# A state-space layer with a SwiGLU branch on one core: five engine streams written with and without a block around them

## The chip, the cores and the metric

The kernel runs on one core of a Trainium2 chip. A core has five engines with an instruction stream each: TensorE (PE in the profile), VectorE (DVE), ScalarE (ACT), GpSimd (POOL) and SyncE (SP). [...] Here SP does no arithmetic: it issues the large transfers to the DMA engines and waits for them. The metric is the device time of one execution in microseconds (us). The kernel before takes 178.64 us (median of 3 runs, 178.61 to 178.97).

## The reference

The input x has 2048 rows of 512. Each row is normalised, and the result goes through two branches whose outputs are added to x:

```python
def _A_ref(x, ...):                       # diagonal complex state space
    Lam_bar = jnp.exp(dt * Lam)           # dt = exp(log_dt)
    B_bar = ((Lam_bar - 1.0) / Lam)[:, None] * Bmat
    Bu = jnp.einsum("bld,pd->blp", x + 0j, B_bar)
    for t in range(L):
        h = Lam_bar[None, :] * h + Bu[:, t, :]
        hs.append(h)
    y = 2.0 * jnp.einsum("blp,dp->bld", hseq, Cmat).real + x * Dskip[None, None, :]
    return y

def _B_ref(x, w_gate, w_up, w_down):
    g = _silu(x @ w_gate)
    u = x @ w_up
    return (g * u) @ w_down

xn = _layernorm(x, axis=-1)
return x + _A_ref(xn, ...) + _B_ref(xn, w_gate, w_up, w_down)
```

There are 512 complex states, and the hidden width of the SwiGLU branch is 1376. Inputs and output are bfloat16.

## The kernel before

The 2048 rows are handled in four chunks of 512. For each chunk VectorE or ScalarE normalises the rows, the rows are transposed (by TensorE in the first chunk, by DMA later), TensorE multiplies them by the gate and up weights (line 807, and line 835 for the first six gate tiles of chunk 0) and by the two parts of B (line 952), ScalarE takes the results out of PSUM (lines 820, 902, 956), VectorE multiplies gate and up (line 904), rotates the states, scans them over time (line 994) and rotates them back, and TensorE adds both branches into one PSUM bank with the down weights (line 1041) and the C weights (line 1054). At the end of a row tile VectorE adds the residual (line 1066) and SP issues the transfer of the tile to the output (the helper at line 438). The last row tile of the last chunk is cut into columns of 256, 128 and 128, so the last addition is 128 columns wide and the last transfer 256.

Nothing is issued directly while this is written down. Every operation is entered into a graph as a task with an engine, its reads, its writes and an estimated cost. At the end `_schedule` orders the tasks of each engine (TensorE and SP keep the order in which they were entered), and `_plan` gives every task the semaphore level it signals and the waits it needs. `_emit` (line 263) then goes through one engine's list and writes each task's waits and its instructions to that engine. A wait that can't ride on an instruction is an instruction of its own (line 266).

The transfers to the output that nobody waits for share one semaphore. `_plan` returns it with its last level as `end_sem, end_lvl`, and SP waits for that level after its last task; this is the kernel's only wait for its own output. The other four engines have no last wait of that sort.

All five lists are written inside a block object, opened at line 306 before the first buffer is laid out. Its five decorated functions (lines 1137 to 1156) each open a section of the program for one engine. A block adds three things: a branch on each engine from the main section into its own section, a branch from there to a common closing section, and in this closing section a barrier of all five engines. The barrier has two sides. ACT, PE, DVE and SP each execute a DRAIN, which raises a gathering semaphore once that engine's earlier work is complete, and then wait for a release; POOL drains, waits until the gathering semaphore has been raised four times, and then raises the release semaphore by four. The profile puts these instructions at line 305, the line of the `with` statement.

A barrier of the same make stands at the start of the program. It belongs to the making of the program object (line 1170), after four small memsets of constants, and has nothing to do with the block. Behind it come, on each engine, the first tasks: on SP and ACT the first transfers (line 438), on PE a run of matmuls on constants (line 508), on POOL memsets (from line 488).

ScalarE's table of activation functions is loaded by an instruction that the program gets when it is completed, ahead of the first activation (line 501).

Of the kernel before, what the change touches and what calls it, by code (L numbers as in the profile page):

```python
# [262 lines left out]
def _emit(eng_obj, stream):  # L263
    for t in stream:
        for sem, val in t.waits:
            eng_obj.wait_ge(sem, val)
        inst = t.fn(eng_obj)
        if t.sem is not None and (t.nsig or t.dma):
            inst.then_inc(t.sem, 16 if t.dma else 1)


def bass_parallel_sum__ssm_conv_s5__swiglu_ffn__prompt_kernel(
# [30 lines left out]
    g = _Graph()  # L303
    es = ExitStack()
    with es:
        block = es.enter_context(nc.Block())

        def sb(name, shape, dt):
            return es.enter_context(nc.sbuf_tensor(name, shape, dt))

# [173 lines left out]
        def loads_wd():  # L484
# [17 lines left out]
              name="act_warm", est=220, prio=1e6)  # L502
# [628 lines left out]
        streams = _schedule(g.tasks, engs)  # L1131
# [2 lines left out]
        eng_sems = {e: new_sem("sem_" + e) for e in engs if e != "sp"}  # L1134
        end_sem, end_lvl = _plan(g.tasks, streams, new_sem, eng_sems)

        @block.sync
        def _(e):
            _emit(e, streams["sp"])
            e.wait_ge(end_sem, end_lvl)  # L1140

        @block.tensor
        def _(e):
            _emit(e, streams["pe"])

        @block.scalar
        def _(e):
            _emit(e, streams["act"])

        @block.vector  # L1150
        def _(e):
            _emit(e, streams["dve"])

        @block.gpsimd
        def _(e):
            _emit(e, streams["pool"])


# [26 lines left out]
```

## Time and profile before

| | |
|---|---|
| median of 3 runs | 178.64 us (178.61 to 178.97) |
| the profiled execution: its own time | 178.72 us |
| the profiled execution: first to last instruction of the program (span) | 177.0 us |
| granted TensorE clock, mean | 1.000 |
| TensorE matmuls, busy | 173.4 us, 98% of the span |
| VectorE, busy | 162.0 us, 92% |
| ScalarE, busy | 101.4 us, 57% |
| GpSimd, busy | 15.1 us, 9% |
| instructions in the trace | 2634 |

The span runs from the first instruction of the program on any engine, at 0.0, to the end of the last one. The execution's own time is longer, because it also covers what the runtime does around the program; the page has no rows for that part. In the rows, an engine's name with a q (SPq, PEq) stands for its sequencer: branches, drains, semaphore waits and the issuing of transfers are done there, take no time on the engine itself, and are not counted as busy. "x" with a number is how often a row's instruction occurs.

### The profile page before, as it was taken

What the parts mean: (1) busy time and instruction counts of PE and PEld (TensorE: products, weight loads), DVE (VectorE), ACT (ScalarE), POOL (GpSimd) and SP (SyncE); (2) the same over time, 40 slices, a digit from 0 to 9 for tenths busy, and PEclk for the clock granted to TensorE, in tenths of its full rate; (3) what the DMA queues carried; (4) which work ended last, traced back from release to release, by engine and by line L of the source; (5) the groups of instructions that cost most, each with busy time, mean ns of one, the idle gap of its engine ahead of it and who ended that gap; (6) DMA issues with size and microseconds to landing.
All of it is one profiled execution on the core that took longest, in us unless ns stands there. A gap on an engine that the chain in (4) does not pass through costs nothing.

```text
span 177.0 us, 2634 instructions
## 1 busy us (share of the span) xinstructions
PE 173.4 (98%) x948; PEld 86.5 (49%) x956; DVE 162.0 (92%) x342; ACT 101.4 (57%) x201; POOL 15.1 (9%) x38
## 2 busy tenths in 40 slices
PE   8999999999999999999999999999999999999994
PEld 2884644455444444446444444445544444444743
DVE  3687899999989979999999999999999999999983
ACT  4679999999998739896598500620666610000000
POOL 6630500000000280000000000000000000000000
DMA  5999669793000700002008000001110000001012
GB/s 149 267 362 250 118 122 171 181 343 131 0 4 0 148 0 0 0 16 77 32 0 150 0 4 0 0 0 59 59 33 0 2 0 0 0 4 59 30 59 89
DMA packets 25092, 12.91 MB, mean 73 GB/s; under 512 B 17304, under 2 KB 25080, under 8 KB 25080
## 3 DMA queue, kind: packets, MB, share of 16 engines
q1 hardware_dynamic: 25056, 12.75, 28.4%
q8 instruction: 7, 0.11, 0.3%
q14 instruction: 5, 0.04, 0.1%
q10 hardware_dynamic: 24, 0.00, 0.0%
HBM read 6.46 MB, written 2.10 MB: 48 GB/s over the span
## 4 chain that ended last, share of the span: by engine, by line
PE 98%; issue 0%; DVE 0%
PE pb L807 36%; PE pb L1041 21%; PE pb L952 16%; PE pb L1054 16%; PE pb L835 3%; PE pb L917 3%; PE pb L508 2%; PE pb L642 1%; DVE osb L1066 0%; PE pb L517 0%
## 5 line engine op out<-in xcount | busy, mean ns | idle before, releaser
L807 PE MATMUL pb<-xnT,wgu 128*128 128x512 bf16 x296 | 64.7, 379 | 0.0
L807 PEld LDWEIGHTS pb<-xnT,wgu 128*128 128x128 bf16 x296 | 28.9, 98 | 33.7
L994 DVE TENSOR_TENSOR_SCAN vq<-sm,car,vq 128x512 bf16<-128x512 f32 x32 | 39.7, 1274 | 0.1
L1041 PE MATMUL pb<-wd,hT 128*128 128x512 bf16 (+3 forms) x194 | 38.1, 355 | 0.2
L1041 PEld LDWEIGHTS pb<-wd,hT 128*128 128x128 bf16 (+1 forms) x198 | 18.5, 98 | 19.9
L952 PE MATMUL pb<-xnT,BT 128*128 128x512 bf16 x128 | 28.1, 379 | 0.0
L1054 PE MATMUL pb<-W,hss 128*128 128x512 bf16 (+2 forms) x140 | 27.8, 355 | 0.2
L956 ACT ACTIVATE u_sb<-pb 128x512 bf16<-128x512 f32 x32 | 18.6, 594 | 13.2 <-PE pb L952 12.4
L902 ACT ACTIVATE uf<-pb 128x512 bf16<-128x512 f32 x40 | 23.5, 606 | 4.3 <-PE pb L807 2.7
L820 ACT ACTIVATE sg<-pb 128x512 bf16<-128x512 f32 x34 | 20.4, 600 | 2.8 <-PE pb L807 2.6
L1054 PEld LDWEIGHTS pb<-W,hss 128*128 128x128 bf16 x144 | 13.5, 98 | 14.2
L952 PEld LDWEIGHTS pb<-xnT,BT 128*128 128x128 bf16 x128 | 12.5, 98 | 15.1
L904 DVE TENSOR_TENSOR hT<-sg,uf 128x512 bf16<-128x512 bf16 x40 | 16.5, 418 | 2.1 <-ACT uf L902 1.3
L1066 DVE TENSOR_TENSOR osb<-pb,x_sb 128x512 bf16<-128x512 f32 (+2 forms) x18 | 11.2, 627 | 1.7 <-PE pb L1054 1.2
L985 DVE TENSOR_TENSOR scrA<-u_sb,cosT 128x1024 bf16<-128x1024 bf16 x16 | 11.0, 687 | 0.6 <-ACT cosT L772 0.5
L988 DVE TENSOR_TENSOR scrA<-u_sb,sin 128x1024 bf16<-128x1024 bf16 x16 | 11.0, 687 | 0.0
L1004 DVE TENSOR_TENSOR scrA<-vq,sin 128x1024 bf16<-128x1024 bf16 x16 | 11.0, 687 | 0.0
L1000 DVE TENSOR_TENSOR scrA<-vq,cosT 128x1024 bf16<-128x1024 bf16 x16 | 11.0, 685 | 0.0
L990 DVE TENSOR_TENSOR vq<-scrA 128x1024 bf16<-128x1024 bf16 x16 | 10.7, 688 | 0.0
L1009 DVE TENSOR_TENSOR hss<-scrA 128x1024 bf16<-128x1024 bf16 x16 | 10.6, 686 | 0.0
L685 POOL TENSOR_TENSOR sm<-sm 128x4 f32<-128x4 f32 x13 | 5.5, 442 | 39.3 <-ACT sm L706 38.9
L599 ACT ACTIVATE xn_sb<-x_sb,ve,rstd 128x512 bf16<-128x512 bf16 x8 | 6.2, 812 | 2.5 <-DVE ve L597 2.5
(87 smaller groups left out, 132.8 us busy)
## 6 DMA issues: line engine op xcount, KB each, us to landing
out_dram<-osb SPq DMA_DIRECT2D x15, 128.0 KB, 1.7
x_sb<-in_A_x_dram SPq DMA_DIRECT2D x3, 512.0 KB, 4.5
wd<-in_B_w_down_dram SPq DMA_DIRECT2D x1, 1280.0 KB, 8.4
wgu<-in_B_w_gate_dram SPq DMA_DIRECT2D x4, 192.0 KB, 3.5
wgu<-in_B_w_up_dram SPq DMA_DIRECT2D x1, 768.0 KB, 6.8
wgu<-in_B_w_gate_dram SPq DMA_DIRECT2D x1, 608.0 KB, 8.0
wgu<-in_B_w_up_dram SPq DMA_DIRECT2D x1, 608.0 KB, 9.7
x_sb<-in_A_x_dram SPq DMA_DIRECT2D x4, 128.0 KB, 2.1
```

Of the source, the lines that this page charges most:

```text
L807: inst = e.matmul(pbank[0:fs, bk, :].rearrange("p (j t) -> p j t", j=4), lhsT=w[:, kt, i * 128:i * 128 + fs], rhs=xnT[:, c % 2, :, kt, :], ...
L820: g.add("act", lambda e, sl=sl, bk=bk, fs=fs: e.activation(out=sg[0:fs, sl, :], in_=pbank[0:fs, bk, :], func=AF.Silu), reads=BK(bk), write ...
L902: g.add("act", lambda e, ul=ul, bk=bk, fs=fs: e.activation(out=uf[0:fs, ul, :], in_=pbank[0:fs, bk, :], func=AF.Identity), reads=BK(bk), w ...
L904: g.add("dve", lambda e, sl=sl, ul=ul, fs=fs, i=i, hb=hb: e.tensor_tensor(out=hT[0:fs, hb, i, :], in0=sg[0:fs, sl, :], in1=uf[0:fs, ul, :] ...
L952: inst = e.matmul(pbank[:, bk, :].rearrange("p (j t) -> p j t", j=4), lhsT=BT[:, ri, kt, pt * 128:(pt + 1) * 128], rhs=xnT[:, c % 2, :, kt ...
L956: last_uev[0] = g.add("act", lambda e: e.activation(out=u_sb[:, us, ri, :], in_=pbank[:, bk, :], func=AF.Identity), reads=BK(bk), writes=[ ...
L985: g.add("dve", lambda e, sl=sl, U=U, Cb=Cb: e.tensor_tensor(out=pr2[:, sl, 0], in0=U, in1=Cb, op=ALU.mult), reads=ru + rdt, writes=[("pr", ...
L988: g.add("dve", lambda e, sl=sl, Usw=Usw, S2=S2: e.tensor_tensor(out=pr2[:, sl, 1], in0=Usw, in1=S2, op=ALU.mult), reads=ru + rdt, writes=[ ...
L994: g.add("dve", lambda e, sl=sl, ri=ri, pt=pt, rr=rr, c=c: e.tensor_tensor_scan(out=vq[:, sl, 1, ri, :], data0=rr[:, pt:pt + 1].to_broadcas ...
L1041: inst = e.matmul(pbank[:, bk, 0:nc_], lhsT=hT[0:fs, hb, i, lt * 128:(lt + 1) * 128], rhs=wd[0:fs, i, c0:c0 + nc_], start=(i == 0), stop=F ...
L1054: inst = e.matmul(pbank[:, bk, 0:nc_], lhsT=hss[:, hb, pt, ri, lt * 128:(lt + 1) * 128], rhs=W12[:, ri, pt, c0:c0 + nc_], start=False, sto ...
L1066: g.add("dve", lambda e, bk=bk, a=a, os_=os_, o0=o0, c0=c0, nc_=nc_: e.tensor_tensor(out=osb[:, os_, o0:o0 + nc_], in0=pbank[:, bk, 0:nc_] ...
```

## The change

The block goes, and with it its five sections. After the streams have been planned, they are written one after the other into the main section of the program, each to its engine; SP's comes last, followed by the same wait for the outputs as before. A wait on SP with no branch behind it is an instruction of its own.

```diff
     with es:
-        block = es.enter_context(nc.Block())
-
         def sb(name, shape, dt):
...
         end_sem, end_lvl = _plan(g.tasks, streams, new_sem, eng_sems)
 
-        @block.sync
-        def _(e):
-            _emit(e, streams["sp"])
-            e.wait_ge(end_sem, end_lvl)
-
-        @block.tensor
-        def _(e):
-            _emit(e, streams["pe"])
...
-        @block.gpsimd
-        def _(e):
-            _emit(e, streams["pool"])
+        for name, eng in (("pool", nc.gpsimd), ("act", nc.scalar), ("pe", nc.tensor), ("dve", nc.vector)):
+            _emit(eng, streams[name])
+        _emit(nc.sync, streams["sp"])
+        nc.sync.wait_ge(end_sem, end_lvl)
```

The tasks, their order on each engine, their semaphores and waits, the buffers and the barrier at line 1170 are as before. The order in which the engines' streams are written has no meaning on the chip, since each engine has its own stream.

More of the change, by code (lines that the diff above doesn't have):

```diff
@@ L1135, in bass_parallel_sum__ssm_conv_s5__swiglu_ffn__prompt_kernel @@
         end_sem, end_lvl = _plan(g.tasks, streams, new_sem, eng_sems)
-        @block.sync
-        def _(e):
-            _emit(e, streams["sp"])
-            e.wait_ge(end_sem, end_lvl)
-        @block.tensor
-        def _(e):
-            _emit(e, streams["pe"])
-        @block.scalar
-        def _(e):
[L1148 to L1152, printed above, removed]
-        @block.gpsimd
-        def _(e):
-            _emit(e, streams["pool"])
+        for name, eng in (("pool", nc.gpsimd), ("act", nc.scalar), ("pe", nc.tensor), ("dve", nc.vector)):
+            _emit(eng, streams[name])
+        _emit(nc.sync, streams["sp"])
+        nc.sync.wait_ge(end_sem, end_lvl)
 _INS = ['A_x', 'A_Lambda_re', 'A_Lambda_im', 'A_B_re', 'A_B_im', 'A_C_re', 'A_C_im', 'A_log_dt', 'A_Dskip', 'B_x', 'B_w_gate', 'B_w_up', 'B_w_down']
```

## The prediction

> **What bounds the kernel now.** I read the page's busy times and its chain of waits first, then the last pieces of that chain, then everything after them. The page:
>
> ```profile
> span 177.0 us, 2634 instructions
> PE 173.4 (98%) x948; PEld 86.5 (49%) x956; DVE 162.0 (92%) x342; ACT 101.4 (57%) x201; POOL 15.1 (9%) x38
> PE 98%; issue 0%; DVE 0%
> ```
>
> The chain that ended last is 98% TensorE. Nothing in the change touches a matmul, its order or a wait in front of one, so these 173 us stay and the question is what lies before the first matmul and behind the last one. Pieces of the chain in order of time (start, duration, what: TensorE's first transposition, a gap, the end), and then busy time by engine in three stretches, the last of which begins where the chain's matmuls are over:
>
> ```profile
> 5.00 0.23 PE pb L642
> ...
> 57.86 0.05 issue
> ...
> 169.47 5.18 PE pb L1054 x39
> 174.65 0.02 issue
> 174.68 0.29 DVE osb L1066
> ```
>
> ```profile
> 40.00:174.60 134.60, 134.18 (x678) 64.66 (x683) 129.61 (x259) 67.73 (x134) 4.92 (x10) 1.00 0.11 29
> 174.60:177.00 2.40, 0.04 (x1) 0.00 (x0) 0.29 (x1) 0.00 (x0) 0.00 (x0) 1.00 0.30 93
> ```
>
> TensorE is busy to 174.65, VectorE adds the last 128 columns to 174.97, and for the last 2 us of the span no engine computes. What fills them is in the timeline of SP, in the row of landing times for the output, in SP's own waits, and in the instructions of line 305, the closing section of the block:
>
> ```profile
> 174.99 0.33 SPq L438 DMA_DIRECT2D out_dram<-osb  x1
> DMA to landing us min/median/max: 1.6/1.7/1.7
> SPq L305 <- DMA out_dram<-osb: 1.2, 1, 1.2
> ```
>
> ```profile
> L305 POOLq EVENT_SEMAPHORE  x2: 17/17/17, 176.8 to 176.9; - x2
> L305 POOLq DRAIN  x1: 301/301/301, 65.8 to 65.8; - x1
> L305 ACTq DRAIN  x1: 626/626/626, 141.7 to 141.7; - x1
> L305 PEldq DRAIN  x1: 1302/1302/1302, 173.4 to 173.4; - x1
> L305 DVEq DRAIN  x1: 328/328/328, 174.7 to 174.7; - x1
> L305 SPq COMPARE_BRANCH  x1: 33/33/33, 176.6 to 176.6; - x1
> L305 SPq DRAIN  x1: 13/13/13, 176.7 to 176.7; - x1
> L305 SPq EVENT_SEMAPHORE  x1: 17/17/17, 176.9 to 176.9; - x1
> L305 ACTq EVENT_SEMAPHORE  x1: 17/17/17, 176.9 to 176.9; - x1
> L305 DVEq EVENT_SEMAPHORE  x1: 21/21/21, 176.9 to 176.9; - x1
> L305 PEldq EVENT_SEMAPHORE  x1: 51/51/51, 176.9 to 176.9; - x1
> ```
>
> (Durations are minimum, median and maximum in ns, then the first and last start.) The last transfer is issued at 174.99 and lands 1.6 us later, at 176.6; there SP's branch, which carries the wait for the outputs, gets through. Then the barrier runs by itself: SP drains at 176.7, POOL has its four signals at 176.8 and releases at 176.9, the others leave at 176.9, PE last after 51 ns, at 177.0. The four other engines had drained at 65.8 (POOL), 141.7 (ACT), 174.7 (PE: 173.4 and 1.30 us) and 175.0 (DVE: 174.7 and 0.33). So the barrier waits for SP alone, and its cost is what follows the landing: 177.0 − 176.6 = 0.4 us.
>
> **The change, part by part.**
>
> *The closing barrier.* All eleven rows of line 305 go. The four drains up to 175.0 lie under the landing of the last transfer and cost nothing; on the path are the branch, SP's drain, POOL's two steps and the way out, together the 0.4 us. SP's branch becomes a plain wait. Its price is that of the same instruction in the rows above, 17 ns. So the end of the span comes at about 176.6 + 0.02, and the term is −0.4 + 0.02 = −0.38 us. Since starts are shown to a tenth, both ends of it are off by up to 0.05: −0.3 to −0.5. The wait itself must stay, and nothing stands behind it on SP. The drains hid nothing: the output's last addition signals SP by its own semaphore, and the transfer starts at 174.99 whether DVE drains or not.
>
> *The branches at the beginning.* Each engine goes from the barrier at line 1170 to its first task. The rows of that barrier, and the first transfers of SP:
>
> ```profile
> L1170 POOLq EVENT_SEMAPHORE  x2: 17/17/17, 0.6 to 0.7; - x2
> L1170 SPq DRAIN  x1: 7/7/7, 0.0 to 0.0; - x1
> L1170 DVEq DRAIN  x1: 10/10/10, 0.1 to 0.1; - x1
> L1170 POOLq MOVE  x1: 35/35/35, 0.1 to 0.1; - x1
> L1170 ACTq DRAIN  x1: 8/8/8, 0.1 to 0.1; - x1
> L1170 PEldq DRAIN  x1: 8/8/8, 0.3 to 0.3; - x1
> L1170 SPq EVENT_SEMAPHORE  x1: 17/17/17, 0.7 to 0.7; - x1
> 0.79 1.35 SPq L438 DMA_DIRECT2D x_sb<-in_A_x_dram  x3
> 2.19 0.91 SPq L438 DMA_DIRECT2D wgu<-in_B_w_gate_dram  x2
> ```
>
> Line 305 has one branch row in all, SP's at 176.6; the nine others that a block stands for have none. Between the release at 0.7 and the first transfer at 0.79 there is room for less than 0.1 us, and two transfers follow each other on SP at 0.05 us too (0.79 + 1.35 = 2.14, next at 2.19). I take 0. The bound is −0.07: this start feeds the first x tile, the statistics and TensorE's first real work, so all of it would reach the end. A loss is excluded, as nothing is put there.
>
> [...]
>
> *The table of activation functions.* It is loaded ahead of the first activation. Should it now be put ahead of the barrier at 1170, nothing follows: the 1.28 us lie before the first x tile, for which ScalarE waits another 1.0 us.
>
> ```profile
> 1.38 1.28 ACT L501 ACT_TABLE_LOAD   x1 [1.38 <-PEq L1170]
> ACT junk L552 <- DMA x_sb<-in_A_x_dram: 1.0, 1, 1.0
> ```
>
> *What lies around the span.* The profiled execution took 178.72 us, 1.72 more than its span. No row covers that part, but it begins when engines leave the program, and this the change moves. Before, all five leave within 0.1 us of 176.9. After, POOL is gone at 66, ACT at 142, PE at 174.7 and DVE at 175.0, and only SP comes at 176.6: the others have 1.6 us or more for whatever each of them does on its way out up to the point where all must meet. The nearest row for such a spread is the opening of the program: coming out of the runtime's opening, SP is at its first instruction at 0.0, DVE, ACT and POOL at 0.1, PE at 0.3. SP is the quickest, PE the latest. If leaving is like entering, the meeting behind the program waited for PE, 0.3 us after SP's readiness, and now waits for SP alone. I take −0.3. The bounds: 0, if each engine's way out is as quick as SP's; and −0.7, the whole time that SP stood in the opening barrier until all had met (first row below), if the closing one is as long and all but SP's last step is now done early.
>
> ```profile
> SPq L1170 <- PEq L1170: 0.7, 1, 0.7
> ```
>
> [...]
>
> *Sum.* −0.38 + 0 − 0.3 = −0.68. Against the profiled execution: 178.72 − 0.68 = 178.04. That execution is 0.08 above the median of the runs, so against the median 178.64 − 0.68 = 177.96. All bounds together: −0.3 to −1.27 (0.5, 0.07 and 0.7), thus 177.37 to 178.34.
>
> **Rivals.**
>
> *A: the time around the span doesn't move.* The meeting behind the program starts with SP, or every engine is ready as soon as SP is. Then only the barrier is saved: 178.64 − 0.38 = 178.26. For it: no row shows that part, and engines that come early may do nothing there but stand and wait. Against it: the 0.3 us between SP and PE at the opening.
>
> *B: the change doesn't do what it says.* The barrier is put back when the program is completed (as the table load is put in), or the runtime closes each stream with the same steps in the gap. Then 178.64 stays. For it: the barrier at 1170 shows that such a barrier comes without the kernel asking. Against it: that one belongs to the opening, and line 305 names the block as the maker of the other.
>
> *C: slower, by instruction loading on PE.* The streams become shorter by a few instructions, so they are cut in other places when they are loaded in pieces during the run:
>
> ```profile
> q8 instruction: 7, 0.11, 0.3%
> q14 instruction: 5, 0.04, 0.1%
> ```
>
> Queue 8 brings 7 packets of 0.11 MB in all, 0.3% of 16 engines' span: 0.003 × 16 × 177.0 / 7 = 1.2 us each. With 948 matmuls and 956 weight loads that is 58 bytes an instruction, so the queue is PE's. If a piece now comes late, PE stands still, and PE is the chain. One piece exposed in full gives 177.96 + 1.2 = 179.16, all seven 177.96 + 8.4 = 186.4. It decides from 0.68 us of standing still, a little over half a piece. Against it: on the chain "issue" has 0%, in pieces of 0.05 us at most, so all seven come well ahead now, and a cut that moves by a few of some 1,900 instructions doesn't change how far ahead.
>
> **How the numbers follow.** The forecast 177.96 has a chance of 0.65, A 0.20, B 0.08, C 0.07. A difference of 0.2% is 0.36 us, about what a measurement of this kernel can tell from no change; faster means below 178.28. The forecast gives 0.65 of faster; A lies on the line at 178.26, and I give it 0.12 faster and 0.08 the same. With B the same is 0.16, faster 0.77, slower 0.07. The range: the bounds of the forecast, from 177.5 (all of them at once at their ends are unlikely), up to 178.4, which takes in A with its rounding. It leaves out B and C and a little at the low end, under 0.2.
>
> **What would show it.** *The barrier:* line 305 has no rows, SP's last row is a wait of some 17 ns at 176.6, and the span ends there, near 176.6 instead of 177.0. Any drain or release after 176.6 would be B. *The beginning:* the first transfer at 0.79 and TensorE's first transposition (5.00) where they were; 0.05 earlier throughout would be the branches. *Around the span:* time less span was 1.72; 1.4 is the forecast, 1.7 is A, 1.0 the other bound. *Loading:* a pause of PE near 1 us, with "issue" as its cause, would be C. I am wrong if matmul pieces of the chain get longer or gaps in it appear: nothing in the sum accounts for either.

## The result, and the profile after

The change takes 177.88 us (median of 6 runs, 177.81 to 178.19) against 178.75 us before (6 runs, 178.61 to 178.97): 0.87 us less. The ratio is 0.9954, with a 95% interval of 0.9941 to 0.9966. In five of the six executions the span is 176.5 or 176.6 us; the profiled one is the sixth, with a span of 176.9 us and a time of 178.19 us. It is read here with that in mind, and a second profile of the same kernel follows as the first experiment. Of the executions reported further down, one of the eleven with the barrier put back took 384.74 us (span 383.0, granted clock 1.000); nothing on record shows why, and it is left out of that kernel's ratio and of its time less span.

The page's first lines and its instruction queues, after the change:

```profile
span 176.9 us, 2631 instructions
PE 174.1 (98%) x956; PEld 86.9 (49%) x956; DVE 162.0 (92%) x342; ACT 101.5 (57%) x201; POOL 15.0 (8%) x38
q8 instruction: 7, 0.11, 0.3%
q14 instruction: 5, 0.04, 0.1%
```

The engines do the same work (the page before counts 948 matmuls where this one counts 956, but the tasks are the same and the weight loads are 956 in both, so the trace before lacks eight matmul records), and the streams are loaded in as many pieces as before. Then SP at both ends: in its timeline (start, duration) the first transfers and the last one, among its waits the one for the output, and in the list of instructions of line 1138 the only row left behind the landing:

```profile
0.79 1.35 SPq L436 DMA_DIRECT2D x_sb<-in_A_x_dram  x3
2.19 0.91 SPq L436 DMA_DIRECT2D wgu<-in_B_w_gate_dram  x2
...
175.33 0.33 SPq L436 DMA_DIRECT2D out_dram<-osb  x1
```

```profile
SPq L1138 <- DMA out_dram<-osb: 1.2, 1, 1.2
```

```profile
L1138 SPq EVENT_SEMAPHORE  x1: 17/17/17, 176.9 to 176.9; - x1
```

The opening is where it was, 0.79 us. At the end the last transfer goes out at 175.33, lands 1.6 us later at 176.9, SP's wait takes 17 ns, and the span is over. Before, 0.4 us came behind the landing. So the barrier has left the span, yet the span of this execution is only 0.1 us shorter, because its last transfer is issued 0.34 us later (175.33, before 174.99). Where that comes from shows in the chain of this execution, in its first 8 us:

```profile
5.00 0.79 PE pb L640 x4
5.79 0.17 PE pb L833
5.96 0.15 PE pb L640
6.12 0.43 PE pb L833 x4
6.54 0.32 PE pb L640 x3
6.86 0.73 PE pb L833 x13
7.59 0.22 PE pb L640 x4
7.81 2.35 PE pb L833 x42
```

and in the same place before:

```profile
5.73 0.17 PE pb L835
5.90 0.13 PE pb L642
6.03 0.22 PE pb L835 x4
6.26 0.17 PE pb L642 x3
6.42 0.83 PE pb L835 x13
7.25 0.22 PE pb L642 x4
7.47 2.35 PE pb L835 x42
```

From 6.1 to 6.9 us seven matmuls (x4 and x3) take 107 ns each (0.43 + 0.32 = 0.75 us) where they took 56 ns before (0.22 + 0.17 = 0.39 us): 0.36 us more. Another 0.09 us was lost ahead of them (6.12 against 6.03), and 0.10 us was regained in the thirteen behind them (0.73 against 0.83). From 7.8 us on both run at 56 ns (2.35 us for 42), and the 0.34 us (7.81 against 7.47) are carried along to the end. In this execution TensorE's matmuls came down to 56 ns about 0.8 us later (at 6.86, before at 6.03). Is that the change or the execution? The first experiment asks.

### The profile page after: what moved, and what is told of

The parts are those of the page before. It is cut to its first block, busy times and chain, and to the rows that moved or that the text cites. A ratio compares the mean times of both kernels' runs of the same rounds, so it can differ in the third digit from the quotient of the medians.

```text
span 176.9 us, 2631 instructions
## 1 busy us (share of the span) xinstructions
PE 174.1 (98%) x956; PEld 86.9 (49%) x956; DVE 162.0 (92%) x342; ACT 101.5 (57%) x201; POOL 15.0 (8%) x38
## 4 chain that ended last, share of the span: by engine, by line
PE 98%; DVE 0%; issue 0%
PE pb L805 36%; PE pb L1039 22%; PE pb L1052 16%; PE pb L950 16%; PE pb L833 3%; PE pb L915 3%; PE pb L506 2%; PE pb L640 1%; DVE osb L1064 0%; PE pb L515 0%
## 5 line engine op out<-in xcount | busy, mean ns | idle before, releaser
L1039 PE MATMUL pb<-wd,hT 128*128 128x512 bf16 (+3 forms) x198 | 38.8, 355 | 0.0
L1052 PE MATMUL pb<-W,hss 128*128 128x512 bf16 (+2 forms) x144 | 28.3, 355 | 0.0
```

The costliest lines, as they stand in the source:

```text
L1039: inst = e.matmul(pbank[:, bk, 0:nc_], lhsT=hT[0:fs, hb, i, lt * 128:(lt + 1) * 128], rhs=wd[0:fs, i, c0:c0 + nc_], start=(i == 0), stop=F ...
L1052: inst = e.matmul(pbank[:, bk, 0:nc_], lhsT=hss[:, hb, pt, ri, lt * 128:(lt + 1) * 128], rhs=W12[:, ri, pt, c0:c0 + nc_], start=False, sto ...
```

## The experiments

Two theories were put against each other. M (meeting): behind the program the engines meet in the runtime's closing part, and what the change gains outside the span comes from four engines being there early. P (program): without a block the program itself runs differently, and the moment at which the engines leave has no part in it. "Time less span" is an execution's own time less its span; the page gives spans to 0.1 us, so medians over the executions are used. It was 1.73 us before (27 executions, 1.69 to 1.81) and is 1.285 us after (6 executions, 1.25 to 1.31).

**The change once more.** No edit.

> The changed kernel once more, unaltered. Question: the profiled execution of the change had a span of 176.9 us, with TensorE's chain 0.33 us longer before 6.9 us than in the kernel before; five others had 176.6. Theory M (the engines' meeting behind the program): the 0.33 us belong to that one execution, so here the span is 176.6 us, the time 177.9 us, and what lies around the span 1.3 us, as against 1.75 before. Rival P (the program itself runs differently without a block): the 0.33 us in the opening come back, span 176.9 us.

Measured: 177.89 us (5 runs, 177.79 to 178.12), ratio 0.9959 (0.9946 to 0.9971). The profiled execution has a span of 176.6 us, and time less span is 1.29 us in the median. Pieces of its chain, and the row of its wait:

```profile
6.42 0.82 PE pb L833 x13
7.47 2.35 PE pb L833 x42
...
174.67 0.29 DVE osb L1064
```

```profile
L1138 SPq EVENT_SEMAPHORE  x1: 17/17/17, 176.6 to 176.6; - x1
```

The 13 matmuls start at 6.42 and the last addition at 174.67, as before the change (6.42 and 174.68). So the 0.34 us belong to single executions and not to the change. (The profile of the kernel with TensorE late, further down, has the same two slow pieces, 0.43 and 0.32 us, and a span of 177.0.) The kernel before varies as much, its spans in this series going from 176.8 to 177.4 us; whether for the same reason isn't shown, since it has one profile. M held.

**The barrier back, without a block.**

```diff
         nc.sync.wait_ge(end_sem, end_lvl)
+        nc.all_engine_barrier()
```

> No block and no branches, but the barrier of all five engines is put back behind the streams. M: the barrier takes 0.25 to 0.3 us behind SP's wait (drain, collecting, release, PE's 51 ns) and the engines leave together again, so the time around the span goes back to 1.7 us: span 176.85, time 178.6 us, within 0.15 of before; the rest, some 0.1 us, is SP's branch. P: only the barrier's own time comes back, around the span stays at 1.3 us: 178.2 us.

Measured: 178.69 us (11 runs), ratio to before 0.9998 (0.9989 to 1.0007), time less span 1.75 us. Four of the rows of the barrier:

```profile
L1139 POOLq EVENT_SEMAPHORE  x2: 17/17/17, 176.7 to 176.8; - x2
L1139 SPq DRAIN  x1: 7/7/7, 176.7 to 176.7; - x1
L1139 SPq EVENT_SEMAPHORE  x1: 17/17/17, 176.8 to 176.8; - x1
L1139 PEldq EVENT_SEMAPHORE  x1: 51/51/51, 176.9 to 176.9; - x1
```

The barrier alone brings back all that a measurement can tell, inside the span and outside of it. By the trace's records to the nanosecond, SP's drain starts 0.061 us after the start of its wait here (176.698 after 176.637); before, with the branch, it was 0.163 us (176.744 after 176.581). P, which expected 178.2 us, falls.

**All five wait, no barrier.**

```diff
         nc.sync.wait_ge(end_sem, end_lvl)
+        for eng in (nc.tensor, nc.scalar, nc.gpsimd, nc.vector):
+            eng.wait_ge(end_sem, end_lvl)
```

> No block, no barrier, but all five engines wait for the output's semaphore at the end of their streams, as SP does. M: span 176.6 us as in the change, but all leave at the same moment, so around the span it is 1.7 us as before: 178.3 us; this is 0.4 us faster than before and 0.45 slower than the change. P: the four waits lie under SP's and cost nothing: 177.9 us.

Measured: 178.47 us (11 runs), ratio 0.9985 (0.9976 to 0.9994), time less span 1.77 us.

```profile
L1140 ACTq EVENT_SEMAPHORE  x1: 17/17/17, 176.5 to 176.5; - x1
L1140 POOLq EVENT_SEMAPHORE  x1: 17/17/17, 176.5 to 176.5; - x1
L1140 DVEq EVENT_SEMAPHORE  x1: 21/21/21, 176.5 to 176.5; - x1
L1140 PEldq EVENT_SEMAPHORE  x1: 51/51/51, 176.5 to 176.5; - x1
```

Here no barrier stands anywhere and the span ends with the landing, at 176.5 us; all engines get through at the same moment, and time less span is what it was before. The expected 178.3 us were met by the profiled execution (178.26); the median is 0.2 higher, and the spans of this group lie at 176.7 in the median. So about half of the gain, some 0.5 us (1.77 against 1.285), is the head start of the four others, and not the barrier's own work. P, which expected 177.9 us, falls here too.

**One engine late at a time.** Four kernels, each with a wait on one further engine; first TensorE:

```diff
         nc.sync.wait_ge(end_sem, end_lvl)
+        nc.tensor.wait_ge(end_sem, end_lvl)
```

> As the change, but TensorE too waits for the output's semaphore at its end; the other three leave early. M, with the engines passing a token one after the other, PE first and SP last, some 35 to 45 ns a step: PE is on its way for some 0.2 us, then four steps follow that the change had behind it already, 0.15 us in all, against SP's own 0.13 us: 0.2 to 0.35 us slower than the change, 178.1 to 178.2 us. If the engines are simply counted and PE is no slower than SP on its way out: 177.9 us. P: 177.9 us.

Measured: 178.30 us (11 runs), ratio 0.9977 (0.9968 to 0.9986), time less span 1.50 us, 0.215 more than the change. The median holds 0.2 us of longer spans besides (176.8), so the 178.1 to 178.2 us were not met, while the difference between what follows the landing in the records below, 1.751 us (178.666 − 176.915) against 1.458 in the change (178.365 − 176.907), is 0.29 us and lies where M put it. That the engines are simply counted, at no cost (177.9 us), falls with it.

Its profile, and that of all five waiting, made the next question: the trace's semaphore records show one semaphore that is stepped again and again after the program, first by one engine after the other. With all five late, the third step hung by 0.28 us. So the same edit followed on GpSimd, ScalarE and VectorE:

```diff
+        nc.gpsimd.wait_ge(end_sem, end_lvl)
```

> As the change, but GpSimd too waits for the output's semaphore at its end. With all five late, the third step of the closing chain came 0.28 us after the second, where TensorE alone late had it 0.04 us after; so one engine is about 0.55 us on its way out. Theory G: it is GpSimd. Then its lateness alone brings back nearly all of what all five together cost, 0.45 to 0.5 us: time less span 1.75 us, time 178.3 to 178.4 us. Rival S: it is ScalarE, and GpSimd costs 0.1 us at most: time less span 1.3 to 1.4 us, 177.9 to 178.0 us.

```diff
+        nc.scalar.wait_ge(end_sem, end_lvl)
```

> As the change, but ScalarE too waits for the output's semaphore at its end. G: ScalarE is about as quick on its way out as SP, and two or three steps of some 0.04 us follow it: 0 to 0.15 us more than the change, time less span 1.3 to 1.45 us, 177.9 to 178.05 us. S: 0.45 to 0.5 us more, time less span 1.75 us.

```diff
+        nc.vector.wait_ge(end_sem, end_lvl)
```

> As the change, but VectorE too waits for the output's semaphore at its end. Both theories put it next to last, one step of 0.02 us ahead of SP: in the change its step came 0.15 us after its last instruction, SP's 0.14 us after SP's. So 0 to 0.1 us more than the change: time less span 1.3 to 1.35 us, 177.9 to 178.0 us. If any late engine costs the same, it is 0.45 us more, as with all five.

| late besides SP | median, us | ratio to before (95%) | time less span, us | more than the change |
|---|---|---|---|---|
| none (the change) | 177.88 | 0.9954 (0.9941 to 0.9966) | 1.285 | |
| VectorE | 178.00 | 0.9966 (0.9952 to 0.998) | 1.35 | 0.065 |
| ScalarE | 178.03 | 0.9966 (0.9955 to 0.9978) | 1.435 | 0.15 |
| TensorE | 178.30 | 0.9977 (0.9968 to 0.9986) | 1.50 | 0.215 |
| GpSimd | 178.45 | 0.9986 (0.9977 to 0.9995) | 1.785 | 0.50 |
| all four | 178.47 | 0.9985 (0.9976 to 0.9994) | 1.77 | 0.485 |

The last three kernels of one late engine (VectorE, ScalarE, GpSimd) ran on another chip than TensorE late and all four; the kernel before, beside them there, took 178.70 us (16 runs) with a time less span of 1.745, so the two series can be compared. The last column is against the 1.285 us of the change throughout. GpSimd alone costs as much as all four together: theory G held, S fell, though the median of 178.45 lies 0.05 us above the range that G gave. The times of ScalarE and VectorE late lie within what was expected; VectorE's 0.065 us is less than the tenth to which spans are given. What the row of its wait shows is innocent, 17 ns at the same moment as SP's:

```profile
L1139 POOLq EVENT_SEMAPHORE  x1: 17/17/17, 176.6 to 176.6; - x1
L1138 SPq EVENT_SEMAPHORE  x1: 17/17/17, 176.6 to 176.6; - x1
```

The time passes behind it, where there are no instruction rows. The trace's records of that one semaphore (number 2; in us from the span's start, one profiled execution each) show it directly. "Through" is when the wait for the output gets through on SP, and in the kernels without a barrier a late engine's wait follows within 0.012 us of it. 1 to 5 are the first five steps, the turn is the sixth, and twelve more follow up to the last:

```
kernel          through   1       2       3       4       5       turn      last of all
before          176.581   177.204 177.239 177.450 177.494 177.518 177.615   178.906
change          176.907   175.147 175.182 175.220 175.451 177.057 177.101   178.365
barrier back    176.637   177.152 177.186 177.398 177.441 177.464 177.562   178.828
all five wait   176.451   176.705 176.739 177.018 177.062 177.085 177.183   178.443
TensorE late    176.915   177.169 177.203 177.241 177.285 177.308 177.405   178.666
ScalarE late    176.817   175.055 176.952 176.990 177.035 177.058 177.155   178.420
GpSimd late     176.631   174.906 174.940 177.198 177.242 177.265 177.363   178.630
VectorE late    176.455   174.695 174.729 174.768 176.634 176.657 176.754   178.023
```

The steps come one after the other, and each engine made late holds up its own and all behind it: TensorE is first, ScalarE second, GpSimd third, VectorE fourth, SP fifth. From the wait that lets it go, an engine needs on its way to its step 0.25 us (TensorE, 177.169 − 176.915), 0.14 (ScalarE, 176.952 − 176.817), 0.57 (GpSimd, 177.198 − 176.631), 0.18 (VectorE, 176.634 − 176.455), 0.15 (SP in the change, 177.057 − 176.907). GpSimd's length doesn't hang on the wait that was added: with a barrier its last instruction is the release, at 176.861 before and at 176.809 with the barrier back, and its step comes 0.589 us later both times. From the turn on everything takes 1.26 to 1.29 us in all eight kernels. An execution's own time is 0.17 to 0.19 us shorter than the last of these records in all eight (before, 178.72 against 178.906), so a last step that comes later is a longer execution by as much. In the change four of the five steps are done at 175.451, while the last transfer is still on its way.

## Why the prediction was right

**The closing barrier, −0.38 us.** Right. In the second profile of the change and in the kernel before, the last transfer lands at the same 176.6 us; the span ends there instead of at 177.0. The wait costs the 17 ns that were taken from SP's row. To the nanosecond, SP's wait gets through at 176.581 before and at 176.565 in that profile, and the spans end at 176.966 and 176.582.

**The branches at the beginning, 0.** Right: by the trace's records SP leaves the barrier at the start of the program (line 1170, 1152 after) at 0.706 and starts its first transfer at 0.791, before and after, so the branches that went there cost no time that these records show. The one branch that has a row, SP's at the end, cost more than its 33 ns. From "through" to the turn is 1.034 us before (177.615 − 176.581) and 0.925 with the barrier put back without a block (177.562 − 176.637), so with the branch in place of a plain wait it is 0.11 us more, most of it (0.102) ahead of SP's drain. That was inside the 0.4 us and needed no term.

**Around the span, −0.3 us.** The sign and the place were right, the size was too small, and the engine was the wrong one. It measured 0.45 us in the medians (1.73 to 1.285). That 0.3 came as near as it did is luck: it was the lateness of another engine, at another place. I took the size from the opening of the program, where TensorE comes 0.3 us after SP and GpSimd 0.1, and concluded that the meeting waits for TensorE. Leaving is not like entering: TensorE late costs 0.215 us, GpSimd late 0.50. All four late don't cost the sum of the four single costs (0.93), but only the largest, as the engines are on their way side by side until each one's step is due: with all four late, GpSimd's step comes 0.567 us after the wait gets through (177.018 − 176.451), as it does with GpSimd late alone (177.198 − 176.631). 0.45 lies inside the bounds given for this term, 0 to 0.7.

**The sum.** −0.38 + 0 − 0.45 = −0.83 us by these terms, −0.87 in the medians, −0.68 predicted. What the term around the span lacked, 0.15 us, is the larger part of the 0.19 us. The predicted 177.96 us is nevertheless only 0.08 above the measured median, and the range holds it, because the median before moved the other way by 0.11 (178.64 in the three runs shown, 178.75 with three more): this too is luck. The records of the semaphore give the whole at once. From "through" to the last step is 2.325 us before (178.906 − 176.581) and 1.458 after (178.365 − 176.907), 0.867 us less, which is the gain in the medians. Of it 0.37 us lies before the end of the span, 0.47 between there and the turn, and 0.03 behind the turn.

**The rivals.** A (the time around the span doesn't move) is refuted by time less span, and its mechanism is refuted with it: the engines need time before they meet, GpSimd 0.57 us of it. B (the barrier stays or is put back): line 1138 is the last row, and no drain follows. C (instruction loading): as many pieces as before, and no gap in the chain near 1 us; that the seven pieces of queue 8 are TensorE's was an estimate from their size, and no row names their engine. The profiled execution did have matmul pieces that got longer, which the prediction named as a sign of being wrong; the second profile of the same kernel doesn't have them, so they aren't the change's.

The meeting of all engines, which the prediction took for granted, shows in these records. The closing part begins with it: in all eight kernels the turn comes 0.04 to 0.10 us after the fifth step, however late an engine made that (177.101 against 177.057 in the change, 176.754 against 176.657 with VectorE late). The records of other semaphores, one step each, come only behind the turn: 249 of them from 177.630 on before, 236 from 177.177 on after. Next to nothing of what follows the turn was gained; up to the last step it is 1.291 us before and 1.264 after. The way to this meeting is a cost of its own, it differs between engines by a factor of four (0.14 us for ScalarE, 0.57 for GpSimd), and it can lie under the last transfer: in the change four steps are done at 175.451, and the wait for that transfer gets through at 176.907.

## What to carry to other kernels

Look at what lies between the landing of the last output and the end of the execution: here it was a barrier of 0.4 us and 0.45 us of engines setting out together for a meeting that four of them could have reached early. Let one engine wait for the output and the others leave when their work is done, GpSimd above all, and put the last wait on an engine that is quick on its way out and comes late in the order of the meeting (SP here). That is drawn from this one kernel, and none of the runs has its only last wait on another engine than SP. The gain of 0.87 us lies behind the landing of the last transfer, so my estimate is that it counts for more in a shorter kernel; no run here shows another length.

## What the runs showed of the hardware that was not expected

GpSimd, whose wait at the end of the program is as short as SP's and ScalarE's (17 ns), is 0.57 us on its way out, against 0.14 to 0.25 us for the four others. What it does in that time no row shows, and the runs leave it open.

The moment from which TensorE takes 56 ns a matmul of 128 columns moves from one execution to the next and moves the time by some 0.3 us (spans of 176.9 and 176.6 us): in one profile of the changed kernel it is 107 ns from 6.1 to 6.9 us, in the other 55 to 63 ns from 6.0 us on (0.22 us for 4 at 6.03, 0.82 for 13 at 6.42), with a granted clock of 1.000 in both. Why it moves, no run here shows. For comparing two single profiles of this kernel it means that a difference of 0.3 us in the span is not yet a difference between the kernels.
